# Fused attention, routed experts and tanh-shrink: the router's pieces at other score blocks, the values' high part on GpSimd

## The chip, the cores and the metric

One NeuronCore of a Trainium2 chip runs the whole program. The metric is the time of one execution on the device, in microseconds; of the kernel before there are three such times and one profiled execution. PE is TensorE, DVE VectorE, ACT ScalarE, POOL GpSimd, SP the engine that issues most DMAs.

## The reference, cut to what matters

```python
def _attn_ref(q, k, v):                     # B, H, S, D = 4, 8, 1152, 64
    q_pool = q.reshape(B, H, S // 2, 2, D).mean(axis=3)
    scores = 1/sqrt(D) * np.matmul(q_pool, k.transpose(0, 1, 3, 2))
    scores = scores - np.max(scores, axis=-1, keepdims=True)
    attn = np.exp(scores); attn = attn / (np.sum(attn, axis=-1, keepdims=True) + 1e-09)
    return np.matmul(attn, v)
...
x = attn_out.transpose(0, 2, 1, 3).reshape(2304, 512)
do_compute = x @ w_skip > 0                 # the router: which tokens, and which expert
e_idx = np.argmax(x @ w_gate, axis=1)
...
y = x + gate_w * (relu(x @ w1[e]) @ w2[e])  # 8 experts
h = y @ w_in; out = (h - np.tanh(h)) @ w_out
```

The change lies wholly in the attention and in the router's share of it.

## The kernel before

**Batches and steps.** The 32 heads are worked off as 16 pairs, n = 0 to 15. `Attention.run` (L426) gives each pair one batch of 18 steps; a step is one block of 128 keys of one head (`st` in the code). In a step TensorE first does the twelve short matmuls of `av` (L299) for the block of six steps earlier (`LAG = 6`), then the two score matmuls of `exact` (L247, L248), at steps 1, 6, 10 and 15 the short score matmuls of `rest` for the last 64 queries, then 0 to 2 matmuls of `maxu` (L187, each 384 keys wide), which find the row maxima for the pair two batches ahead. `MAXU` says how many in which step.

**Who reads what.** ScalarE turns each score block into `ph` (f16, L236) and `p` (f32, L237). GpSimd, in 14 of the 18 steps, makes the low part `pl = p - ph` (L242); VectorE does it in the four steps of `DVE_LO`. VectorE also reduces every `maxu` result (L188). Each pair's inputs are prepared one or two batches ahead by steps that the table `PREP` sets: `v1b`, the high part of the values (`vh = f16(1024 v)`, 128x1152) at step 6, and `v2b`, the low part (`vl = 1024 v - vh`, L153 on VectorE) at step 9; `k2b`, the same of the keys, near step 15. `ENG` says which engine does which. VectorE's preparations wait in the list `bg`, and `behind` takes one after each `maxu`.

**Rings of buffers.** Score blocks rotate through three PSUM buffers (`ps_ex`). Another three (`ps_mx`) are shared by everything else: the `maxu` results, the transposed row maxima of `maxrow2` (L216) and the router's two pieces. A tile of that ring can be written when the tile three places earlier has been read.

**The router's pieces.** When a pair's output is complete (step 5 of the next batch, then four VectorE instructions taken one by one behind the `maxu`), `on_pair` appends the router's pieces of that pair to the list `todo`, which happens in step 7. They are: `first` (four transposes, L545, copied to `r_xt` by ScalarE, L548); in every second quarter of the work, where a pair touches five token tiles in place of four, one more `first` of one transpose (copied by VectorE, L550); `second` (L555: four or five matmuls, two records each in the trace, then VectorE's L560 or L558); and some DMAs of SP (zeros into `ys`, rows of x to `xd`). At the end of each step, one piece is taken if the step is in `SIDE`:

```python
if self.todo and st in (self.LASTSIDE if n == NP - 1 else self.SIDE):
    self.todo.pop(0)()
```

```python
MAXU = (2, 0, 2, 1, 1, 2, 1, 2, 1, 2, 2, 1, 2, 1, 1, 2, 2, 2)
SIDE = (3, 4, 5, 8, 13, 17)
PREP = {-6: ("q1",), -4: ("k1b",), -3: ("k2b",), -1: ("kt",), 0: ("q2",), 1: ("q3",), 2: ("qt",),
        4: ("kc",), 6: ("v1b",), 9: ("v2b",)}
```

So before, in a four-tile batch (pairs 0 to 3 and 8 to 11, whose pieces run in batches 1 to 4 and 9 to 12), `first` is in step 8 and `second` in step 13; in a five-tile batch (5 to 8 and 13 to 15) the pieces are in steps 8, 13 and 17. After the attention come `route`, the experts and the dense layer; their code is the same in both kernels.

Of the kernel before, what the change touches and what calls it, by code (L numbers as in the profile page):

```python
# [27 lines left out]
class Attention:  # L28
# [62 lines left out]
    def prep(self, n, i):  # L91
        if n >= self.NP:
            return
        nc, s, eng = self.nc, self.st[n], self.ENG.get((n, i)) or self.ENG.get(i)
        if i == "q1":
# [215 lines left out]
            self.final(n, h)  # L311

    AVG = (3, 5)
    SIDE = (3, 4, 5, 8, 13, 17)
    LAST_LO = (0, 1, 2, 4, 6, 9, 10, 11, 13, 14, 16, 17)
    LAST_HI = (0, 1, 2, 5, 7, 9, 12, 14, 16)
    LO0 = (9, 10, 12, 13, 14, 16)
# [2 lines left out]
    def final(self, n, h):  # L320
# [17 lines left out]
        if h == 1 and self.on_pair:  # L338
# [4 lines left out]
    PREP = {-6: ("q1",), -4: ("k1b",), -3: ("k2b",), -1: ("kt",), 0: ("q2",), 1: ("q3",), 2: ("qt",),  # L343
            4: ("kc",), 6: ("v1b",), 9: ("v2b",)}

    ENG = {"k1b": "act", "k2b": "dve", "v1b": "act", "v2b": "dve", "k10": "act", "k11": "act", "k20": "dve", "k21": "dve", "q1": "pool", "q2": "act", "q3": "dve",
# [85 lines left out]
    def run(self):  # L432
# [5 lines left out]
        for n in range(NP):  # L438
            for st in range(18):
# [25 lines left out]
                if st == (self.ROW[1] if n else self.ROW0[2]):  # L465
                    self.maxrow2(n + 1)
                if self.todo and st in (self.LASTSIDE if n == NP - 1 else self.SIDE):
                    self.todo.pop(0)()
# [21 lines left out]
class Router:  # L490
# [27 lines left out]
    def setup(self):  # L518
# [13 lines left out]
        for a in range(2):  # L532
            G.memset(self.least[:, a:a + 1], float(max(j for b, j in Experts.SIDE if b == a) + 1))

# [248 lines left out]
class Experts:  # L783
# [6 lines left out]
    SX, S1, S2 = 2.0 ** 8, 2.0 ** 4, 2.0 ** 8  # L790
    SIDE = {(0, 1): 2, (0, 2): 2, (0, 3): 2, (0, 4): 2, (1, 1): 2, (1, 2): 2, (1, 3): 2}

# [10 lines left out]
    def setup(self, ctx, inv, wide):  # L803
# [8 lines left out]
        self.groups, i = {}, 0  # L812
        for k, n in self.SIDE.items():
            self.groups[k] = list(range(i, i + n))
# [451 lines left out]
```

## Time and profile before

| | |
|---|---|
| median of 3 runs | 1055.69 us (1053.09 to 1057.06) |
| profiled execution, its own time | 1054.1 us |
| its span, first to last instruction | 1052.5 us |
| PE busy | 944.3 us (90%) |
| DVE busy | 788.6 us (75%) |
| ACT busy | 649.2 us (62%) |
| POOL busy | 543.1 us (52%) |

The shares of the whole span are averages over stages. The attention takes up about the first 460 us, and there the slices of the profile show ScalarE at 9 tenths, PE at 9, VectorE at 8 and 9, GpSimd at 7 and 8; in the dense layer at the end PE alone is at 9. The chain of waits that ended last is followed back only into the experts (about 600 us), so the attention isn't in it, and is read from its own stretches, batch by batch. A batch begins at the first score matmul (L247, 512 wide) of its step 0: batch 3 at 122.77 us, batch 4 at 148.22, batch 7 at 226.81, batch 8 at 253.12.

### The profile page before, as it was taken

What the parts mean: (1) busy time and instruction counts of PE and PEld (TensorE: products, weight loads), DVE (VectorE), ACT (ScalarE), POOL (GpSimd) and SP (SyncE); (2) the same over time, 40 slices, a digit from 0 to 9 for tenths busy, and PEclk for the clock granted to TensorE, in tenths of its full rate; (3) what the DMA queues carried; (4) which work ended last, traced back from release to release, by engine and by line L of the source; (5) the groups of instructions that cost most, each with busy time, mean ns of one, the idle gap of its engine ahead of it and who ended that gap; (6) DMA issues with size and microseconds to landing.
All of it is one profiled execution on the core that took longest, in us unless ns stands there. A gap on an engine that the chain in (4) does not pass through costs nothing. (4 is left out here: it accounts for less than half of the span.)

```text
span 1052.5 us, 25432 instructions
## 1 busy us (share of the span) xinstructions
PE 944.3 (90%) x10249; PEld 703.9 (67%) x10249; DVE 788.6 (75%) x1420; ACT 649.2 (62%) x1224; POOL 543.1 (52%) x478
## 2 busy tenths in 40 slices
PE   5688999999999999948879775999999999999998
PEld 2355666666666666636657453778888888888886
DVE  8677888888888899867979953877666666666654
ACT  4586999999999998835444351444444444444443
POOL 8855888777888887523645622242332323223221
PEclk8898999999999999978989987999999999999999
DMA  7764878855575630039647352211111211212100
GB/s 221 145 155 123 225 185 176 202 125 126 129 180 126 134 99 15 27 127 358 221 162 284 123 190 99 78 50 42 60 52 40 71 41 40 61 31 70 21 21 21
DMA packets 129795, 122.50 MB, mean 116 GB/s; under 512 B 92270, under 2 KB 96878, under 8 KB 128622
## 3 DMA queue, kind: packets, MB, share of 16 engines
q1 hardware_dynamic: 121934, 92.74, 34.0%
q0 software_dynamic: 7712, 27.79, 7.5%
q8 instruction: 91, 1.49, 0.6%
q14 instruction: 58, 0.48, 0.2%
HBM read 74.73 MB, written 19.14 MB: 89 GB/s over the span
## 5 line engine op out<-in xcount | busy, mean ns | idle before, releaser
L242 POOL TENSOR_TENSOR pl<-p,ph 128x512 f16<-128x512 f32 x214 | 265.4, 1258 | 80.6 <-ACT p L237 64.2
L188 DVE TENSOR_REDUCE m<-ps_m 128x1 f32<-128x384 f32 x432 | 222.8, 546 | 32.3 <-PE ps_m L187 30.5
L1095 POOL TENSOR_TENSOR gl<-v,gh 128x512 fp32r<-128x512 f32 x71 | 92.1, 1298 | 271.6 <-ACT gh L1094 267.6
L236 ACT ACTIVATE ph<-ps_e 128x512 f16<-128x512 f32 x279 | 184.3, 660 | 57.2 <-PE ps_e L248 56.0
L1094 ACT CAST gh<-v 128x512 fp32r<-128x512 f32 x72 | 44.5, 618 | 190.1 <-DVE v L1093 190.1
L299 PEld LDWEIGHTS <-ph 128*128 128x128 f16 x2304 | 133.2, 99 | 42.6 <-issue 15.5
L1078 PE MATMUL ps_ch<-xT,wi 128*128 128x256 f16 x576 | 159.0, 276 | 0.7 <-ACT xT L1062 0.7
L1079 PE MATMUL ps_ch<-xT,wi 128*128 128x256 f16 x576 | 158.3, 275 | 0.5 <-DVE xT L1063 0.4
L1080 PE MATMUL ps_ch<-xT,wi 128*128 128x256 f16 x576 | 158.3, 275 | 0.0
L187 PE MATMUL ps_m<-ks,qT 128*128 128x384 f16 (+1 forms) x480 | 124.7, 339 | 24.3 <-DVE m L188 16.3
L237 ACT ACTIVATE p<-ps_e 128x512 f32<-128x512 f32 x211 | 142.7, 676 | 0.0
L299 PE MATMUL ps_a<-vh,pl 128*128 128x65 f16 x1152 | 136.4, 195 | 0.0
L299 PE MATMUL ps_a<-vh,ph 128*128 128x65 f16 x1152 | 136.3, 195 | 0.0
L299 PE MATMUL ps_a<-vl,ph 128*128 128x65 f16 x1152 | 136.2, 195 | 0.0
L1089 DVE SCALAR_TENSOR_TENSOR v<-u,ps_ch 128x512 f32<-128x512 f32 x72 | 49.3, 685 | 113.5 <-ACT t L1087 103.0
L1111 PE MATMUL ps_co<-wo,gh 128*128 128x512 f32 x288 | 119.7, 416 | 0.0
L1113 PE MATMUL ps_co<-wo,gl 128*128 128x512 f32 x288 | 114.0, 396 | 1.0 <-POOL gl L1095 1.0
L247 PE MATMUL ps_e<-qT,ks 128*128 128x512 f16 x288 | 111.2, 386 | 4.0 <-ACT p32r L237 2.0
L248 PE MATMUL ps_e<-qT,kh 65*128 65x512 f16 x288 | 111.6, 388 | 3.4 <-DMA qT<-mt 3.4
L1112 PE MATMUL ps_co<-wo,gh 128*128 128x512 f32 x288 | 113.6, 394 | 0.0
L299 PEld LDWEIGHTS <-pl 128*128 128x128 f16 x1152 | 108.2, 98 | 0.0
L187 PEld LDWEIGHTS <-qT 128*128 128x128 f16 (+1 forms) x480 | 42.2, 102 | 77.0 <-issue 43.9
(222 smaller groups left out, 2158.2 us busy)
## 6 DMA issues: line engine op xcount, KB each, us to landing
v<-in_v_dram SPq DMA_DIRECT2D x16, 576.0 KB
k<-in_k_dram SPq DMA_DIRECT2D x15, 576.0 KB
q<-in_q_dram SPq DMA_DIRECT2D x16, 512.0 KB
raw<-in_moe_w_in_dram SPq DMA_DIRECT2D x8, 1024.0 KB
w1f<-in_moe_w_dram POOLq DMA_DIRECT2D x8, 1024.0 KB, 7.1
w2f<-in_moe_w_dram POOLq DMA_DIRECT2D x8, 1024.0 KB, 8.1
raw<-in_moe_w_out_dram SPq DMA_DIRECT2D x8, 1024.0 KB
ys<-zero SPq DMA_DIRECT2D x5, 1280.0 KB
```

The lines of the kernel that those rows point to most:

```text
L187: nc.tensor.matmul(ps[o, 0:384], w, ks[:, h, c * 384:(c + 1) * 384], start=True, stop=True)
L188: nc.vector.tensor_reduce(out=s["m2"][:, i, c:c + 1], in_=ps[:, 0:384], axis=AX.X, op=ALU.max)
L236: nc.scalar.activation(ph, ps, AF.Exp, scale=2.0 ** -20)
L237: nc.scalar.activation(src, ps, AF.Exp, scale=2.0 ** -20)
L242: (nc.vector if dve else nc.gpsimd).tensor_tensor(out=pl, in0=src, in1=ph, op=ALU.subtract)
L299: self.nc.tensor.matmul(o, x, r, start=first and i == 0, stop=k == NKT - 1 and i == 2, skip_group_check=True)
L1078: nc.tensor.matmul(ps[:, a], self.wi[0][:, w], xh[:, c], start=c == 0, stop=False)
L1079: nc.tensor.matmul(ps[:, a], self.wi[0][:, w], xl[:, c], start=False, stop=False)
L1080: nc.tensor.matmul(ps[:, a], self.wi[1][:, w], xh[:, c], start=False, stop=c == 3)
L1111: nc.tensor.matmul(o, gh[:, a, s], self.wo[0][:, w], start=f == 0, stop=False)
L1112: nc.tensor.matmul(o, gh[:, a, s], self.wo[1][:, w], start=False, stop=False)
L1113: nc.tensor.matmul(o, gl[:, a, s], self.wo[0][:, w], start=False, stop=f == 15)
```

## The change

Two tables of `Attention` change. `SIDE` names other steps, and `v1b` is given to GpSimd (`high` then issues L144, a `tensor_scalar` with the output as before, in place of ScalarE's L140).

```diff
-    SIDE = (3, 4, 5, 8, 13, 17)
+    SIDE = (3, 5, 7, 10, 13, 17)
...
-    ENG = {"k1b": "act", "k2b": "dve", "v1b": "act", "v2b": "dve", "k10": "act", ...
+    ENG = {"k1b": "act", "k2b": "dve", "v1b": "pool", "v2b": "dve", "k10": "act", ...
```

`v1b` without a number for the half is issued in batches 1 to 13, so thirteen instructions move from ScalarE to GpSimd. The pieces of the router go to steps 7 and 10 in a four-tile batch, and to 7, 10 and 13 in a five-tile batch; DMA pieces that followed in step 17 or in step 3 of the next batch now come in 13 and 17.

GpSimd in batch 3, steps 3 to 8 (`pl` and `rl` are low parts of probabilities, `vh` the values' high part), as a piece of the difference:

```order
 L242 TENSOR_TENSOR pl<-p_2373,ph 128x512
+L144 TENSOR_SCALAR vh_144<-v_1582 128x18x64
 L242 TENSOR_TENSOR pl<-p_2399,ph 128x512
 L242 TENSOR_TENSOR pl<-p_2430,ph 128x512
 L242 TENSOR_TENSOR rl_0_159<-p32r,rh_0_158 128x256
```

The new instruction stands between the low parts of steps 4 and 5.

VectorE in batch 3, steps 8 to 13, before (`m_2056` takes the maxima of the pair two ahead, `m_2682` those of the pair after it; `lg` are the router's logits):

```order
L188 TENSOR_REDUCE m_2056<-ps_m 128x1 x3
L153 SCALAR_TENSOR_TENSOR vl_147<-v_1581,vh_144 128x18x64
L188 TENSOR_REDUCE m_2056<-ps_m 128x1 x2
L242 TENSOR_TENSOR rl_1_157<-ps_l,rh_1_156 128x320
L188 TENSOR_REDUCE m_2056<-ps_m 128x1 x2
L188 TENSOR_REDUCE m_2682<-ps_m 128x1
L208 TENSOR_REDUCE mm<-m_2056 128x9
L558 TENSOR_TENSOR lg<-ps_r,lg 128x36
```

And after the change:

```order
L188 TENSOR_REDUCE m_2062<-ps_m 128x1 x3
L153 SCALAR_TENSOR_TENSOR vl_147<-v_1582,vh_144 128x18x64
L188 TENSOR_REDUCE m_2062<-ps_m 128x1
L558 TENSOR_TENSOR lg<-ps_r,lg 128x36
L188 TENSOR_REDUCE m_2062<-ps_m 128x1
L242 TENSOR_TENSOR rl_1_157<-ps_l,rh_1_156 128x320
L188 TENSOR_REDUCE m_2062<-ps_m 128x1 x2
L188 TENSOR_REDUCE m_2688<-ps_m 128x1
L208 TENSOR_REDUCE mm<-m_2062 128x9
```

The reading of `second` (L558) moves from behind the last maximum to right behind the first reduction that follows `vl`.

TensorE in batch 3 (it multiplies with `vh_142`), step 10, as a piece of the difference (`second` is new there):

```order
 L187 LDWEIGHTS qT
 L187 MATMUL ps_m<-ks,qT 128x384
+L555 MATMUL ps_r<-w_81,r_xt 128x9 x4
 L299 LDWEIGHTS ph
 L299 MATMUL ps_a<-vh_142,ph 128x65
```

And step 13 of the same batch, where it is taken away:

```order
 L187 LDWEIGHTS qT
 L187 MATMUL ps_m<-ks,qT 128x384
-L555 MATMUL ps_r<-w_81,r_xt 128x9 x4
 L299 LDWEIGHTS ph
 L299 MATMUL ps_a<-vh_142,ph 128x65
```

In step 10 it stands behind two `maxu` matmuls, in step 13 it stood behind one.

## Rows read from the trace of the kernel before

**Rows 1.** Busy time by stretch: batches 3, 6, 13; us (instructions) of PE, PEld, DVE, ACT, POOL; TensorE's clock, DMA share, GB/s.
```profile
122.77:148.22 25.45, 24.26 (x392) 16.87 (x388) 22.25 (x47) 23.94 (x49) 21.77 (x19) 1.00 0.80 191
...
200.50:226.81 26.31, 24.88 (x394) 17.15 (x391) 23.04 (x48) 24.04 (x48) 21.04 (x19) 1.00 0.54 123
...
380.83:409.38 28.55, 25.56 (x420) 17.81 (x417) 27.60 (x60) 24.06 (x49) 21.02 (x19) 1.00 0.35 85
```

**Rows 2.** Waits in 97.43 to 380.83 (batches 2 to 12): us, times, longest.
```profile
POOL pl L242 <- ACT p L237: 33.2, 59, 1.1
...
PE ps_m L187 <- DVE m L188: 10.2, 18, 1.2
...
PE ps_e L247 <- ACT p32r L237: 1.4, 4, 0.4
```

**Rows 3.** Timeline of TensorE, batch 3, steps 12 to 14: start, us, instruction [idle before].
```profile
139.27 0.35 PE L187 MATMUL ps_m<-ks,qT 128*64 128x384 f16 x2
140.19 0.35 PE L187 MATMUL ps_m<-ks,qT 128*64 128x384 f16 x2 [0.57 <-DVE m L188]
140.86 0.38 PE L247 MATMUL ps_e<-qT,ks 128*128 128x512 f16 x1
...
141.52 1.06 PE L555 MATMUL ps_r<-w,r_xt 128*128 128x9 f32 x8
142.44 0.19 PE L299 MATMUL ps_a<-vh,ph 128*128 128x65 f16 x1
...
142.80 0.38 PE L247 MATMUL ps_e<-qT,ks 128*128 128x512 f16 x1
```

**Rows 4.** Timeline of VectorE, batch 3, steps 10 to 17.
```profile
137.33 2.35 DVE L153 SCALAR_TENSOR_TENSOR vl<-v,vh 128x1152 f16<-128x1152 f32 x1
139.60 1.01 DVE L188 TENSOR_REDUCE m<-ps_m 128x1 f32<-128x384 f32 x2
...
142.62 0.20 DVE L558 TENSOR_TENSOR lg<-ps_r,lg 128x36 f32<-128x36 f32 x1
143.60 0.56 DVE L188 TENSOR_REDUCE m<-ps_m 128x1 f32<-128x384 f32 x1 [0.78 <-PE ps_m L187]
...
147.57 1.41 DVE L153 SCALAR_TENSOR_TENSOR kn<-k,kn 128x1152 f16<-128x1152 f32 x1
```

**Rows 5.** Timeline of TensorE, step 0 of batch 4.
```profile
149.51 0.32 PE L187 MATMUL ps_m<-ks,qT 128*128 128x384 f16 x1 [0.53 <-DVE m L188]
```

**Rows 6.** Timeline of TensorE, step 17 of batch 7 (five tiles).
```profile
251.16 1.28 PE L555 MATMUL ps_r<-w,r_xt 128*128 128x9 f32 x10 [0.41 <-DVE m L188]
```

**Rows 7.** Groups of GpSimd, shapes apart, whole span: xcount | busy us, mean ns | idle before.
```profile
L144 POOL TENSOR_SCALAR vh<-v 128x576 f16<-128x576 f32 x2 | 1.3, 673 | 0.2
```

**Rows 8.** Groups of instructions, batches 2 to 12.
```profile
L140 ACT ACTIVATE vh<-v 128x1152 f16<-128x1152 f32 x11 | 13.7, 1243 | 0.0
```

**Rows 9.** Timeline of GpSimd, batch 3, steps 2 to 10.
```profile
128.35 5.92 POOL L242 TENSOR_TENSOR pl<-p,ph 128x512 f16<-128x512 f32 x5 [0.19 <-ACT p L237]
...
137.30 3.38 POOL L242 TENSOR_TENSOR pl<-p,ph 128x512 f16<-128x512 f32 x2 [0.32 <-ACT p L237]
```

**Rows 10.** Line 153 in 95 to 445 us: duration ns min/median/max, first and last start.
```profile
L153 DVE SCALAR_TENSOR_TENSOR kn<-k,kn x12: 1341/1419/1677, 96.6 to 380.6; 128x1152 f16<-128x1152 f32 x12
...
L153 DVE SCALAR_TENSOR_TENSOR vl<-v,vh x12: 1539/2342/2349, 111.9 to 396.6; 128x1152 f16<-128x1152 f32 x12
```

**Rows 11.** Timeline of SP, batch 3.
```profile
137.16 0.50 SPq L168 DMA_DIRECT2D kh<-ks  x1
145.03 0.81 SPq L225 DMA_DIRECT2D qT<-mt  x1
```

**Rows 12.** Busy time in 88 to 95 us.
```profile
88.00:95.00 7.00, 7.00 (x61) 5.02 (x61) 3.43 (x11) 4.29 (x9) 2.08 (x2) 0.50 0.08 29
```

**Rows 13.** Timeline of TensorE, batch 1, step 13.
```profile
87.60 1.71 PE L555 MATMUL ps_r<-w,r_xt 128*128 128x9 f32 x8
```

**Rows 14.** Timeline of TensorE, step 14 of batch 14.
```profile
428.69 0.27 PE L216 MATMUL ps_t<-ident,mm 128*9 128x128 f32 x1 [1.29 <-DVE mm L208]
```

More of the change, by code (lines that the diff above doesn't have):

```diff
@@ L344 @@
             4: ("kc",), 6: ("v1b",), 9: ("v2b",)}
-    ENG = {"k1b": "act", "k2b": "dve", "v1b": "act", "v2b": "dve", "k10": "act", "k11": "act", "k20": "dve", "k21": "dve", "q1": "pool", "q2": "act", "q3": "dve",
+    ENG = {"k1b": "act", "k2b": "dve", "v1b": "pool", "v2b": "dve", "k10": "act", "k11": "act", "k20": "dve", "k21": "dve", "q1": "pool", "q2": "act", "q3": "dve",
            "v10": "act", "v11": "act", "v20": "dve", "v21": "dve", (0, "k11"): "act", (0, "k21"): "pool",
```

## The prediction

> **What bounds the kernel now.** The change touches the attention alone, so I read the attention batch by batch: first the busy time of each engine in whole batches, then the list of waits over batches 2 to 12, then the timelines of single steps.
>
> A four-tile batch lasts 25.45 us, and in it TensorE is busy for 24.26, ScalarE 23.94, VectorE 22.25, GpSimd 21.77 [rows 1]. All four are nearly full, so the question is who makes whom wait. The list of waits answers it: TensorE waits 10.2 us for the reductions of VectorE (L188) and 1.4 us for ScalarE, while GpSimd waits 33.2 us for ScalarE's results [rows 2]. TensorE sets the pace, at its full clock of 1.00 [rows 1], and loses time where the three buffers of the ring `ps_mx` are all unread. GpSimd has the most room: 25.45 less 21.77 is 3.68 us a batch.
>
> The timelines show where the ring fills. In step 10 VectorE starts `v2b` (vl, 2.35 us), and the reductions behind it start only at 139.60 [rows 4]. TensorE runs on to step 12, places the first pair of L187 at 139.27 and must wait 0.57 us for the second [rows 3]. The same happens in step 0 of the next batch, 0.53 us [rows 5], behind the keys' low part at 147.57 [rows 4]. A five-tile batch lasts 26.31 us [rows 1]; there `second` has ten matmul records, stands in step 17 and waits 0.41 us itself [rows 6].
>
> **The change, part by part.**
>
> *`second` in a four-tile batch, from step 13 to step 10.* Its matmuls take 142.44 less 141.52, so 0.92 us [rows 3]. In step 10 they delay steps 11 and 12 by that, and then TensorE meets the same reductions later. The ring has turned by one tile: the first pair of step 12 now needs the buffer that the second pair needed, and comes at 139.27 + 0.92 = 140.19, which is when that buffer came free before [rows 3]. The second pair needs the buffer of `second`, which L558 (0.20 us [rows 4]) empties right behind that reduction, at about 140.3; the pair comes a pair later (modelled 0.35), at 140.5. So the wait of 0.57 is filled with work that used to stand in step 13. Step 13 begins at 140.86 + 0.92 - 0.57 = 141.21 and is 0.92 shorter: step 14 begins 0.57 earlier. VectorE can follow, since it waited 0.78 us for TensorE just there [rows 4]. The wait in step 0 [rows 5] moves along with the keys' low part and stays. There are seven such batches (2 to 4 and 9 to 12; 25.34 to 25.45 us long): 7 x 0.57 = 4.0 us. Bounds: 0, if VectorE can't follow, and 7 x (0.57 + 0.53) = 7.7, if both waits go.
>
> *Five-tile batches (5 to 8).* Step 10 takes the one transpose, too short to fill the wait, so the first pair of step 12 waits until 140.19 and the second follows 0.35 later. Then `second`, 1.28 less 1.06 longer than the four-tile one [rows 3, 6], stands in step 13 as it does in a four-tile batch now. Such a batch should last 25.45 + 0.35 + 0.22 = 26.02 where it lasted 26.31: 4 x 0.29 = 1.2 us. Bounds: 0 and 4 x (0.29 + 0.57).
>
> *Batch 1.* There `second` ran at a granted clock of 0.50, 1.2 GHz [rows 12], and took 1.71 us [rows 13]. In step 10 it runs at 1.00 and stands ahead of a pile of thirteen L187 that wait for VectorE anyway. The slow stretch ends when it ends, so what comes up in its place is slowed too; I take half of 1.71, 0.85 us (bounds 0 and 1.71).
>
> *Batches 13 to 15.* Batch 13 is VectorE's: 27.60 of 28.55 us busy [rows 1], so at most 0.95 is there; I take 0.4. In step 14 of batch 14 TensorE waits 1.29 us for the row maxima [rows 14]; the five-tile `second`, some 1.1 us, now stands ahead of that wait in step 13; I take 0.6. Together 1.0 (bounds 0 and 0.95 + 1.29).
>
> *`v1b` from ScalarE to GpSimd, thirteen times.* ScalarE loses 1.24 us a batch [rows 8]. TensorE waits for ScalarE only 1.4 us in eleven batches [rows 2], so I take no gain; the bounds are 0 and 13 x 1.24 = 16. GpSimd has never done 1152 columns of this; half as many took 0.67 us [rows 7], so at most 1.35, which the idle 3.68 us cover. Behind it wait the low parts of steps 5 and 6, about 1.3 us later; they were ready near 134.3 [rows 9] and are multiplied six steps after their scores, six times 25.45 / 18 or 8.5 us, so no one notices. `v2b` needs its result at 137.33 [rows 4]; GpSimd makes it from about 131.9, after three of the five low parts that begin at 128.35 [rows 9]. Without that cover the full 1.35 would come on the path, 17.6 us in all.
>
> VectorE's low part of the values takes a median of 2.34 us where the keys' takes 1.34 at best, and the former starts 0.03 us after a low part of GpSimd [rows 4, 9, 10]; both read two tensors from SBUF. The Trainium skill (GPSIMD Engine Reference, "Key points") says that GpSimd shares its SBUF interfaces with VectorE and contends with its instructions that have two SBUF inputs. By that rule `v1b` costs VectorE only if it meets such an instruction; at 131.9 to 133.3 VectorE reduces from PSUM, and the sum stays. Charging VectorE with all of it would give 17.6 us against the change.
>
> *DMAs.* Zero fills and x rows move past L225, the row of maxima, on SP's queue. They wait for nothing late, and between the end of L168's issue and L225 SP has 7.4 us free [rows 11]; nothing is charged.
>
> Sum: 4.0 + 1.2 + 0.85 + 1.0 = 7.05 us off the profiled execution's 1054.1, so 1047.0. The median of the runs shown is 1.6 above that execution; on its scale the forecast is 1048.6, and all times below are on it.
>
> **The rivals.** About 0.5%, 5.3 us, is what a measurement of this kernel can tell from no change; "faster" means below 1050.4.
>
> 1. *VectorE gives nothing back.* If VectorE, not the ring, is the limit from step 10 to step 0, the 0.57 reappears as a longer wait in step 0. For it: all of TensorE's waits end with VectorE [rows 2]. Against it: its idle 0.78 us in between [rows 4]. Only the last terms stay, 1.85: 1053.8.
>
> 2. *`v1b` frees VectorE.* If the delayed GpSimd starts its low part of step 9 behind the start of `v2b`, that instruction falls from 2.35 toward 1.54, its best [rows 10], by 0.8 us. In four-tile batches nothing waits any more; in the four others the wait of 0.57 goes too, 2.3 us, and about half a microsecond each in batches 1 and 13: 1045.3. It takes a `v1b` close to 1.4 us. The Trainium skill's rule above (GPSIMD Engine Reference, "Key points") is what would do it; the spread of 1.54 to 2.35 agrees [rows 10].
>
> 3. *ScalarE was the limit.* It has 1.5 us of idle time in a batch [rows 1]. If TensorE's waits only hid its queue, the 1.24 us come back too, thirteen times a good half of it, some 9 us more: 1039.6. Against it stand the 1.4 us of waits.
>
> 4. *GpSimd becomes the limit: slower.* With 3.68 us of idle time less the 0.57 that a batch gets shorter, it decides from a `v1b` of about 3.1 us, and beyond 3.7 the batch is longer than before. At 4.5 us a batch takes 21.77 + 4.5 = 26.27, 0.82 more than now, 10.7 in thirteen: 1066.4. Only a price of 3.3 times twice the 0.67 of the half [rows 7] would do it.
>
> That the change does less than it says is rival 1 in effect: the pieces aren't spread over more blocks in a four-tile batch, they stand in two as before, three blocks apart.
>
> **How the numbers follow.** Forecast 0.52, rivals 0.22, 0.11, 0.08 and 0.07 in that order. The forecast's own range is 1044.5 to 1052, by the bounds of its terms; a tenth of it or more lies above 1050.4. Faster: 0.9 x 0.52 + 0.11 + 0.08 = 0.66; the same: 0.05 + 0.22 = 0.27; slower: 0.07. The range leaves out the slow rival and the far end of rival 3: 1040 to 1056.
>
> **What would show it.** Right: four-tile batches of some 24.9 us and five-tile ones of 26.0; no wait of TensorE in step 12 of the former; L555 in step 10; L144 of 1.1 to 1.35 us with GpSimd's waits for ScalarE smaller; step 0 still waiting some 0.5. Wrong: a wait of over 1 us in step 0, L144 over 3 us, or a `vl` much shorter than 2.3 us, which is rival 2.

## The result, and the profile after

The changed kernel takes 1044.53 us (median of 4 runs, 1043.07 to 1046.08) where the kernel before, in the same comparison, takes 1055.74 (4 runs): a ratio of 0.9905, 95% interval [0.9882, 0.9928]. The forecast was 1048.6 in a range of 1040 to 1056: faster, as forecast, by 4 us more. The profiled execution of the changed kernel took 1046.08 us and is the longest of its four, so the two profiles differ by 8.0 us where the medians differ by 11.2. The kernel before has only four executions in that comparison; in the next one it has 22, with a median of 1054.28, and against that the difference is 9.8.

The first part of the page (busy time of each engine) and, from a list of groups with shapes apart, the moved instruction (xcount | busy us, mean ns | idle before):

```profile
PE 941.9 (90%) x10249; PEld 704.6 (67%) x10249; DVE 788.5 (75%) x1420; ACT 641.4 (61%) x1211; POOL 557.1 (53%) x491
```
```profile
L144 POOL TENSOR_SCALAR vh<-v 128x1152 f16<-128x1152 f32 x13 | 15.0, 1156 | 1.1
```

Thirteen instructions went from ACT to POOL, at 1.16 us each, and VectorE's sum is the same to 0.1 us. Busy time by stretch, batches 3, 6 and 13 (columns as in [rows 1]):

```profile
119.33:144.02 24.69, 24.16 (x391) 16.82 (x388) 22.14 (x47) 23.22 (x48) 22.84 (x20) 1.00 0.77 193
194.92:221.14 26.22, 24.44 (x395) 17.18 (x392) 23.19 (x48) 23.53 (x48) 22.14 (x20) 1.00 0.63 135
372.31:401.10 28.79, 25.69 (x421) 17.89 (x417) 26.42 (x58) 23.48 (x48) 19.94 (x19) 1.00 0.30 65
```

Against [rows 1] the four-tile batch is 0.76 us shorter, the five-tile one only 0.09, and batch 13 is 0.24 longer. The waits in batches 2 to 12, against [rows 2]:

```profile
POOL pl L242 <- ACT p L237: 13.7, 26, 0.9
PE ps_m L187 <- DVE m L188: 10.4, 15, 1.2
...
PEld ps_r L555 <- DVE m L188: 1.4, 4, 0.3
```

GpSimd's waits for ScalarE's `p` fell from 33.2 to 13.7 us and TensorE's wait for ScalarE is gone, but TensorE waits for VectorE's maxima as long as before (10.2 and 10.4). The total hides a shift, which the timeline of TensorE shows: batch 3 from step 10 on (three rows), step 12 of batch 7, step 0 of batch 8, and batch 13 (the last three):

```profile
133.45 0.95 PE L555 MATMUL ps_r<-w,r_xt 128*128 128x9 f32 x8
...
136.77 0.52 PE L187 MATMUL ps_m<-ks,qT 128*64 128x384 f16 x4
138.04 0.33 PE L187 MATMUL ps_m<-ks,qT 128*128 128x384 f16 x1
...
238.91 0.55 PE L187 MATMUL ps_m<-ks,qT 128*64 128x384 f16 x4 [0.52 <-DVE m L188]
...
249.27 0.32 PE L187 MATMUL ps_m<-ks,qT 128*128 128x384 f16 x1 [1.15 <-DVE m L188]
...
387.92 0.33 PE L545 MATMUL ps_r<-ident,x_all 128*128 128x128 f32 x1 [0.44 <-DVE m L188]
...
391.26 0.35 PE L187 MATMUL ps_m<-ks,qT 128*64 128x384 f16 x2 [0.65 <-DVE m L188]
392.15 0.35 PE L187 MATMUL ps_m<-ks,qT 128*64 128x384 f16 x2 [0.54 <-DVE r_xt L550]
```

In the four-tile batch both pairs of step 12 follow each other without a wait, where there was one of 0.57 [rows 3]. In the five-tile batch the first pair of step 12 still waits, and step 0 behind it waits 1.15 us, where batches 6 to 8 before waited under 0.1 in step 0. A wait of that length was there before the change too, in step 0 of batches 5 and 13, where no `second` stands in step 17 ahead of it; this is batch 5 before:

```profile
175.58 0.32 PE L187 MATMUL ps_m<-ks,qT 128*128 128x384 f16 x1 [1.15 <-DVE m L188]
```

Batch 13 after the change has three waits in steps 10 and 12, one of them for the extra `first` that VectorE copies (L550).

What doesn't move with the steps is `vl`, which stands in front of the maxima. VectorE and GpSimd in batch 3:

```profile
133.96 2.30 DVE L153 SCALAR_TENSOR_TENSOR vl<-v,vh 128x1152 f16<-128x1152 f32 x1
136.18 0.54 DVE L188 TENSOR_REDUCE m<-ps_m 128x1 f32<-128x384 f32 x1
136.65 0.18 DVE L558 TENSOR_TENSOR lg<-ps_r,lg 128x36 f32<-128x36 f32 x1
```
```profile
128.67 1.16 POOL L144 TENSOR_SCALAR vh<-v 128x1152 f16<-128x1152 f32 x1
...
132.77 4.50 POOL L242 TENSOR_TENSOR pl<-p,ph 128x512 f16<-128x512 f32 x3
```

`vl` lasts 2.30 us here (2.35 in [rows 4]); three low parts of GpSimd that need 3.39 us elsewhere need 4.50 beside it.

**Where the 8.0 us between the two profiles are** (from the starts of the batches, the last matmul of the attention, the first one of the experts and the first one of the dense layer, L1078): batches 0 and 1, 78.2 to 75.4 us; batches 2 to 13, 312.0 to 306.5; batches 14 and 15, no change; from the last L299 to the first L889, which is the routing, 22.5 to 20.5; experts, 172.9 to 175.2; dense layer, 400.6 to 400.5. A part that the prediction didn't name, the routing, gave 2.0 us.

### The profile page after: what moved, and what is told of

The parts are those of the page before. It is cut to its first block, busy times and chain, and to the rows that moved or that the text cites. A ratio compares the mean times of both kernels' runs of the same rounds, so it can differ in the third digit from the quotient of the medians.

```text
span 1044.6 us, 25445 instructions
## 1 busy us (share of the span) xinstructions
PE 941.9 (90%) x10249; PEld 704.6 (67%) x10249; DVE 788.5 (75%) x1420; ACT 641.4 (61%) x1211; POOL 557.1 (53%) x491
## 5 line engine op out<-in xcount | busy, mean ns | idle before, releaser
L188 DVE TENSOR_REDUCE m<-ps_m 128x1 f32<-128x384 f32 x432 | 225.5, 548 | 37.4 <-PE ps_m L187 34.7
L236 ACT ACTIVATE ph<-ps_e 128x512 f16<-128x512 f32 x279 | 177.0, 635 | 57.5 <-PE ps_e L248 54.2
L299 PEld LDWEIGHTS <-ph 128*128 128x128 f16 x2304 | 133.4, 99 | 49.7 <-issue 22.6
L1078 PE MATMUL ps_ch<-xT,wi 128*128 128x256 f16 x576 | 158.7, 275 | 0.7 <-ACT xT L1062 0.7
L187 PE MATMUL ps_m<-ks,qT 128*128 128x384 f16 (+1 forms) x480 | 122.7, 338 | 23.9 <-DVE m L188 16.1
L299 PE MATMUL ps_a<-vh,ph 128*128 128x65 f16 x1152 | 136.7, 195 | 0.0
L299 PE MATMUL ps_a<-vh,pl 128*128 128x65 f16 x1152 | 136.6, 195 | 0.0
L299 PE MATMUL ps_a<-vl,ph 128*128 128x65 f16 x1152 | 136.5, 195 | 0.0
L237 ACT ACTIVATE p<-ps_e 128x512 f32<-128x512 f32 x211 | 134.5, 637 | 0.0
L299 PEld LDWEIGHTS <-pl 128*128 128x128 f16 x1152 | 108.4, 98 | 0.0
L187 PEld LDWEIGHTS <-qT 128*128 128x128 f16 (+1 forms) x480 | 42.9, 102 | 68.1 <-issue 34.3
```

The costliest lines, as they stand in the source:

```text
L187: nc.tensor.matmul(ps[o, 0:384], w, ks[:, h, c * 384:(c + 1) * 384], start=True, stop=True)
L188: nc.vector.tensor_reduce(out=s["m2"][:, i, c:c + 1], in_=ps[:, 0:384], axis=AX.X, op=ALU.max)
L236: nc.scalar.activation(ph, ps, AF.Exp, scale=2.0 ** -20)
L237: nc.scalar.activation(src, ps, AF.Exp, scale=2.0 ** -20)
L299: self.nc.tensor.matmul(o, x, r, start=first and i == 0, stop=k == NKT - 1 and i == 2, skip_group_check=True)
L1078: nc.tensor.matmul(ps[:, a], self.wi[0][:, w], xh[:, c], start=c == 0, stop=False)
```

## The experiments

Each row below is one kernel. "Pieces" says in which steps the router's pieces run, "vh" which engine makes the high part of the values. Ratios are to the kernel before on the same chip. Lengths are from the profile: a four-tile and a five-tile batch (batches 3 and 6 or 7; in the kernel before the five-tile batches 5 and 8 take 26.84 and 26.04), batch 13, batches 2 to 13 together, and the routing (last L299 to first L889).

| kernel | pieces | vh | ratio, 95% interval | four | five | 13 | 2 to 13 | routing |
|---|---|---|---|---|---|---|---|---|
| before | old | ACT | 1 | 25.45 | 26.31 | 28.55 | 312.0 | 22.5 |
| the change | new | POOL | 0.9905 [0.9882, 0.9928] | 24.69 | 26.22 | 28.79 | 306.5 | 20.5 |
| side_only | new | ACT | 0.9970 [0.9953, 0.9986] | 24.81 | 26.45 | 28.21 | 307.7 | 22.5 |
| v1b_only | old | POOL | 0.9969 [0.9951, 0.9987] | 25.47 | 26.34 | 29.63 | 313.3 | 21.0 |
| five_early | new, own for five | POOL | 0.9845 [0.9818, 0.9873] | 24.69 | 25.55 | 27.14 | 302.4 | 19.7 |
| maxu_moved | new | POOL | 0.9901 [0.9879, 0.9923] | 24.68 | 25.88 | 28.45 | 304.8 | 20.4 |
| both | new, own for five | POOL | 0.9818 [0.9792, 0.9843] | 24.68 | 25.04 | 26.79 | 299.7 | 20.6 |
| five_early_act | new, own for five | ACT | 0.9891 [0.9864, 0.9918] | 24.81 | 25.55 | 27.01 | 302.7 | 22.4 |
| both_act | new, own for five | ACT | 0.9902 [0.9872, 0.9932] | 24.80 | 25.04 | 26.68 | 300.4 | 21.9 |
| side_from2 | new from batch 2 | POOL | 0.9929 [0.9903, 0.9955] | 24.70 | 26.22 | 28.80 | 306.6 | 20.7 |
| v1b_dve | new | DVE | 0.9911 [0.9884, 0.9938] | 24.75 | 25.55 | 28.50 | 303.9 | 22.5 |
| dve_only | old | DVE | 0.9920 [0.9889, 0.9951] | 24.70 | 25.60 | 28.88 | 304.2 | 23.0 |
| both_dve | new, own for five | DVE | 0.9883 [0.9852, 0.9913] | 24.75 | 25.17 | 27.78 | 301.7 | 22.6 |
| v2b_late | new | POOL | 1.0049 [1.0029, 1.0068] | 25.91 | 26.20 | 31.86 | 317.9 | 20.6 |

**The two edits apart.** `side_only` is the changed kernel with `"v1b": "act"`, `v1b_only` the kernel before with `"v1b": "pool"`.

> The changed kernel with v1b back on ScalarE (only SIDE is new). Theory A (the gain comes from 0.9 us of second's matmuls filling TensorE's wait in step 12, v1b is neutral): four-tile batches of 24.7 to 24.9 us as in the changed kernel, no wait in step 12, time within 3 us of the changed kernel (1042 to 1048). Theory B (ScalarE was the limit and the gain is v1b's): four-tile batches back at about 25.4 us, time within 2 us of the kernel before.

> The kernel before with v1b on GpSimd (SIDE is old). Theory A: four-tile batches stay at 25.4 us with the wait of 0.57 in step 12 and the time is within 2 us of the kernel before. Theory B: the batches shorten by up to 1 us each, the time by 8 to 13 us. If v1b disturbs the low parts of GpSimd (the slow rival) the time rises above that of before.

Medians of 1050.9 and 1051.39 where the kernel before has 1054.28. In the batches the steps do nearly all: with them alone, batches 2 to 13 go from 312.0 to 307.7, and the high part on GpSimd adds 1.2; with the old steps it gives the batches nothing (313.3, since batch 13 is 1.1 longer). The five-tile batch of `side_only` (26.45) is no shorter than before. In ratios the two don't add up: 3 and 3 us apart, 10 together; with intervals of 2 us and more either way, most of that gap may be noise. By the batches theory A holds in both; by the time no theory holds: 1050.9 lies above theory A's 1048, and 1051.39 is 2.9 us under the kernel before, where theory A allowed 2. The routing, which no theory had, gives `v1b_only` 1.5 of these 2.9.

**Own steps for the five-tile batches.** The wait in their step 12 was not filled, because only the one transpose stands in step 10; `five_early` puts `second` there.

```diff
+    SIDE5 = (3, 5, 7, 8, 10, 17)
...
-    if self.todo and st in (self.LASTSIDE if n == NP - 1 else self.SIDE):
+    if self.todo and st in (self.LASTSIDE if n == NP - 1 else self.SIDE5 if n > 4 and (n - 1) // 4 % 2 else self.SIDE):
```

> The changed kernel with the pieces of five-tile batches in steps 7, 8 and 10 in place of 7, 10 and 13, so that second's ten matmul records (1.12 us) and not one transpose follow v2b's start. Theory A: the five-tile batches fall from 26.22 us to about 25.0 and lose the wait in step 12, in all 4 x 1.2 = 5 us less than the changed kernel, plus up to 1 us in batches 13 and 14: 1038 to 1040. If VectorE is the limit in five-tile batches whatever the order (it reads one more tile), they stay above 26 and the time stays at 1044.

Measured 1039.02 us. TensorE's timeline in step 12 of batch 7 has no wait left, and the windows of batches 7 and 13:

```profile
236.26 0.52 PE L187 MATMUL ps_m<-ks,qT 128*64 128x384 f16 x4
```
```profile
217.96:243.51 25.55, 24.30 (x395) 16.90 (x391) 23.08 (x48) 23.44 (x48) 22.16 (x20) 1.00 0.61 128
367.83:394.97 27.14, 25.41 (x420) 17.65 (x417) 25.60 (x58) 23.48 (x48) 19.96 (x19) 1.00 0.32 69
```

0.67 us in each of four batches and 1.65 in batch 13: 4.3 us by the batches, some 6 by the ratio. The time is theory A's, but by another sum: the five-tile batches stay at 25.55, not 25.0, and batch 13 gives more than was expected. What was filled is the wait that the prediction had left standing, and by the means that it described for the four-tile batches. The longer wait in step 0 is still there, in batch 8:

```profile
245.43 0.32 PE L187 MATMUL ps_m<-ks,qT 128*128 128x384 f16 x1 [1.16 <-DVE m L188]
```

**The wait in step 0.** One matmul of the maxima goes from step 0 to step 1.

```diff
-    MAXU = (2, 0, 2, 1, ...
+    MAXU = (1, 1, 2, 1, ...
```

> The changed kernel with one maxu moved from step 0 to step 1 (MAXU begins 1, 1 in place of 2, 0), so that its buffer has been read when it comes. Theory A (the ring behind k2b makes the wait of step 0, VectorE has room): the wait of 0.53 us in step 0 goes (1.3 in five-tile batches), batches shorten by 0.6 to 0.7 us, in all 7 to 10 us less than the changed kernel: 1035 to 1038. If VectorE is the limit from v2b to step 2, the wait reappears in step 1 or 2 and the time stays at 1044.

Measured 1044.07. The wait in step 0 is gone (0.69 us in four-tile batches with the pauses around it), and steps 1 and 2 of those are as much longer, 0.47 and 0.21 us, with new waits for ScalarE of 0.30 and 0.18 us. The waits of TensorE in batches 2 to 12:

```profile
PE ps_l L247 <- ACT p L237: 3.3, 11, 0.3
PE ps_m L187 <- DVE m L188: 2.6, 4, 0.7
PE ps_e L247 <- ACT p32r L237: 2.0, 11, 0.2
```

The four-tile batch keeps its 24.68: ScalarE takes the place of the ring there, so the time is that of the second theory, but the engine behind it isn't VectorE. Only the five-tile batches, whose step 0 waited longer, gain (0.34). Both edits together:

> The kernel with its own steps for the five-tile batches and with one of the maxima's matmuls moved from step 0 to step 1. Moved alone it took away the wait of step 0, which came back in steps 1 and 2, so that four-tile batches kept their 24.68 us and five-tile ones went from 26.22 to 25.88. Theory A (VectorE is behind from the keys' low part on, and both edits take the same wait of the five-tile batches): four-tile batches 24.7, five-tile ones 25.5 to 25.6, batch 13 near 27.1, and a median of 1038 to 1040, as with the first edit alone. Theory B (the waits of step 0 and of step 12 are two): five-tile batches of 25.2 or less and a median of 1036 to 1038.

Measured 1035.13, the best of all: 0.9818 of the kernel before, about 9 us under the change. In the windows of batches 3, 7 and 13 the five-tile batch is 25.04, within 0.36 of a four-tile one; the two waits were two, so theory B is right for them.

```profile
116.81:141.49 24.68, 24.19 (x392) 16.82 (x389) 22.12 (x47) 23.23 (x48) 22.83 (x20) 1.00 0.77 192
216.23:241.27 25.04, 24.46 (x395) 16.98 (x392) 23.04 (x48) 23.22 (x48) 22.11 (x20) 1.00 0.60 131
365.01:391.80 26.79, 25.58 (x420) 17.71 (x417) 25.48 (x58) 23.37 (x48) 19.93 (x19) 1.00 0.32 70
```

**What the high part on GpSimd is worth.** `five_early_act` and `both_act` are those two kernels with `"v1b": "act"`.

> The kernel with its own steps for the five-tile batches, and the values' high part back on ScalarE. In the medians so far the two edits apart gave 3.4 and 2.9 us and both together some 10; in the batches of the profiles the high part on GpSimd is worth 0.12 us in a four-tile batch (24.81 against 24.69) and 0.23 in a five-tile one (26.45 against 26.22), and batch 13 gives 0.6 back. Theory A (what the batches show is all there is): four-tile batches back at 24.81, batches 2 to 13 together 1 to 2 us longer than the 302.4 us with GpSimd, and a median of 1040 to 1042, where it was 1039.0 with GpSimd. Theory B (the two edits need each other somewhere outside of those batches, as the medians suggest): a median of 1044 to 1046, with the loss before batch 2 or behind the attention.

> The same kernel with the values' high part on ScalarE, where the kernel before had it. In it the waits left in steps 1 and 2 are for ScalarE (0.46 and 0.36 us a batch). Theory A (the high part on GpSimd is worth what the batches show): batches up to 0.3 us longer than with GpSimd's 24.68 and 25.04, 1 to 3 us in thirteen, and a median of 1036 to 1038 where GpSimd gave 1035.1. Theory B (it is worth more, outside of those batches, as the medians of the other pairs, 3 to 6 us, suggest): a median of 1039 to 1042 with batches that are hardly longer.

Medians of 1041.46 and 1042.56. In batches 2 to 13 ScalarE costs 0.3 and 0.8 us more than GpSimd, even less than theory A has it; the ratios differ by 0.0046 and 0.0084, some 5 and 9 us with intervals of about 4 us either way, which is theory B's side. (The medians alone put the first, 1041.46, into theory A's range.) Part of what lies outside the batches can be seen. GpSimd at the end of the attention, before and after the change (L836 starts a load of expert weights, L845 the gather of the first expert's rows):

```profile
470.44 0.97 POOL L836 DMA_DIRECT2D w1f<-in_moe_w_dram  x1 [17.27 <-DVE slot L700]
471.71 1.05 POOL L845 DMA_INDIRECT bx<-xd,inv  x1 [0.17 <-issue]
```
```profile
458.61 0.97 POOL L836 DMA_DIRECT2D w1f<-in_moe_w_dram  x1 [13.70 <-DVE kf L608]
459.59 0.12 POOL L695 MEMSET inv<- 128x2 int32 x1
462.21 1.04 POOL L845 DMA_INDIRECT bx<-xd,inv  x1 [2.50 <-DVE slot L700]
```

Before, the load is issued 17.3 us after GpSimd's last low part, and the gather, which the experts wait for, only behind it. After, the load goes out 3.6 us earlier, and the gather as soon as VectorE has made its addresses (`inv`, L699, just ahead of L700). The instructions and their order there are the same. L700 in the first line is the profile's guess and no cause: after the change the same load starts before L700. In all seven kernels that have the high part on GpSimd the idle time is 13.7 us and the routing 19.7 to 21.0; in all seven others it is 17.0 to 17.6 and 21.9 to 23.0, whichever of ScalarE and VectorE has it. In these seven an 8 KB transfer of the instruction queue starts 1.8 to 2.4 us before the late load, in the first seven 1.4 to 1.8 us after it, where GpSimd waits for the addresses anyway. In the late seven the gather starts 1.2 to 1.8 us after L700 ends, in the first seven always 0.21 us after it. Of `side_only`, from 457.7 to 461.6 us, the DMA queues show:

```profile
q1 hardware_dynamic: 324, 0.82, 53.9%
q14 instruction: 1, 0.01, 0.5%
```

So with thirteen instructions more ahead of that place GpSimd doesn't stop before the load, which is worth 2.0 us between the two kernels: the gather is 1.2 us earlier against L700, and the first expert matmul 0.7 earlier against the gather, which isn't explained. That the stop is a wait for instructions to arrive is read from the coincidence of fourteen profiles and isn't shown; no kernel tested it by adding instructions that do nothing.

**Batch 1.** The changed kernel with the old steps in batches 0 and 1:

```diff
-    ... else self.SIDE):
+    ... else self.SIDE if n > 1 else (3, 4, 5, 8, 13, 17)):
```

> The changed kernel with the old steps for the pieces in batches 0 and 1 alone. Theory A (batch 1 is 5.2 us shorter since the router's second piece moved out of its half-clock stretch): batch 1 back at about 35 us, batch 0 as it was, batch 2 beginning near 97 to 99 us, and a median 3 to 5 us over the 1044.5 of the change. Theory B (batches 0 and 1 scatter with where the half-clock stretches fall, since batch 0, whose code is the same, moved by 2.3 us as well): batch 2 begins between 94 and 97.5 us, batch 1 has the waits of the kernel before in its own steps, and the median is within 2 us of 1044.5. Batches 2 to 13 should be as in the change in both, 306.5 us together.

Measured 1045.55, and batch 1 takes 29.61 us, as in the change (30.01): theory B, though batch 2 begins at 93.64, just ahead of its 94. Over all profiles batch 1 takes 29.6 to 35.2 us with its old steps (four kernels) and 28.4 to 31.9 with the new ones (ten), and batch 0, which the edits hardly touch, 43.0 to 45.4. Both kernels have a granted clock of 0.50 (1.2 GHz) near 20 to 27 and 34 to 41 us; then the kernel before has it once more, from 84.8 to 95.0 us, the change twice, from 58.2 to 65.1 and from 85.6 to 89.0. With the old steps batch 1 is the longer the more of it is at clock 0.50: 29.61 us with 3.4 of them, 31.43 with 7.2, 31.73 with 7.4, 35.21 with 10.2 (the kernel before). So the 5.2 us that batch 1 lost between the two profiles can't be put down to the steps, and what these are worth there can't be told.

**The high part on VectorE.** `v1b_dve` is the change with `"v1b": "dve"`, `dve_only` the kernel before with it, `both_dve` the best kernel with it.

> The changed kernel with the values' high part on VectorE, where half of it took 0.73 us, so 1.46 for the whole. It tells what a microsecond of VectorE costs in a batch. Theory A (VectorE sets the pace between the waits of TensorE for its reductions; its idle time elsewhere can't be used): four-tile batches grow by 0.7 to 1.46 us, to 25.4 to 26.1, and the thirteen batches by 9 to 19 us: a median of 1054 to 1063. Theory B (only the ring's two places matter, and VectorE catches up between step 6 and step 10): four-tile batches stay within 0.3 us of 24.69, and the median within 4 us of 1044.5.

> The kernel before (old steps for the router's pieces) with the values' high part on VectorE. In the profiles so far each low part of keys or values on VectorE (L153, 1152 columns) ends 1.21 or 1.22 us after the end of the low part that GpSimd has in hand when it starts, so its length is set by where in GpSimd's instruction it starts; with the high part on VectorE and the new steps, it was 1.46 us in place of 2.30 and 2.12, and the wait of the five-tile batches in step 12 was gone. Theory A (the wait of step 12 is the length of vl, and the pieces only filled it): with vl near 1.5 the old steps lose it too; four-tile batches of 24.8 to 25.0 us, where they had 25.44, five-tile ones of 25.4 to 25.9, where they had 26.3, no wait over 0.3 us in step 12, and a median of 1045 to 1049. Theory B (the wait comes of where the pieces stand): four-tile batches stay at 25.4, five-tile ones at 26.3, and the median at 1051 to 1054.

> The kernel with its own steps for the five-tile batches, with one of the maxima's matmuls moved from step 0 to step 1, and with the values' high part on VectorE in place of GpSimd. Theory A (VectorE has room, since vl is shorter by most of what the high part takes): four-tile batches 24.6 to 24.8 us, five-tile ones 24.9 to 25.1, a median of 1034 to 1037, as with the high part on GpSimd (1035.1). Theory B (without the wait of step 0 VectorE's sum of about 22.7 and 23.8 us a batch is what is left): batches longer by 0.3 or more each, and a median of 1039 or above.

Medians of 1043.5, 1045.41 and 1041.14. `v1b_dve` is theory B's: VectorE gets an instruction more in every batch, and the four-tile batches are only 0.06 longer for it, while its five-tile batches fall from 26.22 to 25.55, and `dve_only`, with the old steps, has batches 2 to 13 in 304.2 us, less than the whole change. The windows of batches 3 and 7 of `dve_only`, then its VectorE and TensorE in batch 3 (step 12 is the four L187):

```profile
121.03:145.80 24.77, 24.13 (x392) 16.88 (x389) 22.49 (x48) 23.30 (x48) 22.13 (x19) 1.00 0.87 197
222.12:247.70 25.58, 24.71 (x394) 17.10 (x391) 22.98 (x49) 23.38 (x47) 21.38 (x19) 1.00 0.58 131
```
```profile
131.76 1.39 DVE L142 TENSOR_SCALAR vh<-v 128x1152 f16<-128x1152 f32 x1
...
135.77 1.35 DVE L153 SCALAR_TENSOR_TENSOR vl<-v,vh 128x1152 f16<-128x1152 f32 x1
```
```profile
137.78 0.52 PE L187 MATMUL ps_m<-ks,qT 128*64 128x384 f16 x4
```

`vl` takes 1.35 us in place of 2.35, so VectorE's sum is 22.49 where it was 22.25, and the wait of step 12 is gone with the old steps too: theory A. Only in batch 13 `vl` takes 2.33 us again, and there step 12 waits 0.83. That wait is the length of `vl`; the new steps had only filled it. `both_dve` falls between its theories: the median is theory B's and the four-tile batches theory A's, but batch 13, where VectorE is busiest, is 1.0 longer than in `both`, five-tile ones 0.13, and the routing 2.0, as wherever GpSimd lacks the thirteen instructions. Batches and routing make 4.0 of the 6 us by which it is slower than `both`.

**`vl` two reductions later.** The changed kernel with one step changed:

```diff
-            4: ("kc",), 6: ("v1b",), 9: ("v2b",)}
+            4: ("kc",), 6: ("v1b",), 10: ("v2b",)}
```

> The changed kernel with the low part of the values (vl) called for in step 10 in place of step 9, which puts it two reductions later in VectorE's order, behind the reading of the router's second piece. Theory A (TensorE's waits follow vl): vl lasts between 1.25 and 2.4 us and ends 1.22 us after the low part that GpSimd has in hand when it starts; the wait of 0.68 us in step 12 of the five-tile batches moves to a later step or goes; four-tile batches of 24.5 to 24.9 us, five-tile ones of 25.5 to 26.2, and a median of 1041 to 1045. Theory B (the wait belongs to step 12's two matmuls, whatever vl does): step 12 still waits 0.6 us or more in the five-tile batches, which stay at 26.2, and the median is that of the change, 1043 to 1046.

Measured 1058.14 us, 1.0049 [1.0029, 1.0068] of the kernel before and 14 us above the change; both theories missed the time. The wait did follow `vl`: step 12 of the five-tile batches has none, and `second` in step 13 waits the 0.52 that step 12 had. But in four-tile batches `vl` now meets GpSimd's L99 and is long again (VectorE, GpSimd and TensorE, batch 3):

```profile
137.90 2.36 DVE L153 SCALAR_TENSOR_TENSOR vl<-v,vh 128x1152 f16<-128x1152 f32 x1
```
```profile
137.63 1.41 POOL L99 TENSOR_TENSOR qs<-q 128x576 f32<-128x576 f32 x1
```
```profile
141.18 0.32 PE L187 MATMUL ps_m<-ks,qT 128*128 128x384 f16 x1 [0.57 <-DVE m L188]
142.29 0.27 PE L216 MATMUL ps_t<-ident,mm 128*9 128x128 f32 x1 [0.79 <-DVE mm L208]
```

The last maxima now stand behind it. In step 14 the matmul of the maxima waits for a buffer, and the row maxima (L208) that TensorE transposes there come late: a chain that had no wait in the change. Four-tile batches are 1.2 longer than in the change, batch 13 3.1.

## Why the prediction was right, point by point

- **The direction and the place were right.** The waits of TensorE behind VectorE's `vl` were the thing to fill, and `second` in step 10 fills the one of step 12 in the four-tile batches. The prediction's term was 0.57 a batch, 4.0 in seven; measured are 0.76 and 5.1. The steps alone give 0.64 (`side_only`), the high part another 0.12, which the prediction set at 0.
- **The five-tile term failed in part**: 1.2 forecast, 0.6 measured, of which 0.6 is batch 5 alone and the other three gain 0.01 together (the prediction took 26.31 for all four, where batches 5 and 8 had 26.84 and 26.04). The wait of step 12 stays, as stated. The step that failed is the next one, "as it does in a four-tile batch now": step 0 waits 1.15 us there, not the 0.53 of [rows 5], since the keys' low part starts later (0.27 us before step 0, against 0.64) and takes 1.67 us in place of 1.42. What makes it start later isn't located. Before, `second` in step 17 had stood in front of that wait and filled it in batches 6 to 8, so moving it away opened a wait elsewhere. Step 0 of batch 5 showed its length before the change; [rows 5] is of batch 4.
- **Batches 13 to 15**: 1.0 forecast, and 0.3 longer measured (batch 13 0.24 longer, batch 14 0.26 shorter, batch 15 0.30 longer). The step "at most 0.95 is there; I take 0.4" failed: VectorE's idle time rose to 2.4 us there, but TensorE's waits for VectorE in steps 10 to 13 of batch 13 only moved. They were 0.50 and 1.12 us before and are 0.44, 0.65 and 0.54 after, the last of them for L550 in the middle of a pile of maxima.
- **Batch 1**: 0.85 forecast, 5.2 shorter in the profile, with 2.3 of it given back in batch 0; `side_from2` shows that the steps there are not needed for it. No run tells whether this term is right.
- **`v1b` at nothing** was right for VectorE and GpSimd: L144 takes 1.16 us (1.1 to 1.35 forecast), and no one waits for it. As a term of the sum it was wrong by 1.2 us in the batches and by 2.0 in the routing, which the prediction didn't look at because its code is the same.
- **The sum is in part luck.** It was 7.05 us, and the profiles place 7.4: 5.1 in the four-tile batches, 0.6 in the five-tile ones, -0.3 in batches 13 to 15 and 2.0 in the routing. The second and third of these are 1.9 short of the forecast, the first is 1.1 over it, batch 1 can't be told from scatter, and the routing, which wasn't in the sum, made up for the rest.
- **Rivals.** 1 fell: VectorE gives the time back in four-tile batches. 2 has the right mechanism, with another cause than `v1b` on GpSimd: `vl` stays at 2.30 and 2.12 us in the change, but where it is shortened (`dve_only`) the waits go as the rival said. 3 fell in its size: 1.2 us came back in the batches, about the 1.4 us of waits that stood against it. 4 fell: 1.16 us against the 3.1 that it needs.
- **What stays open.** The ratios make the high part on GpSimd worth 3 to 9 us in four pairs of kernels, with intervals of 2 to 4 us either way; batches and routing show 0.2 to 3.2. The rest, if it is more than noise, lies in the start, the experts or the dense layer and isn't located: these differ by 4 to 6 us over the fourteen profiles (batch 2 begins at 91.8 to 97.4 us, the experts take 171.0 to 176.4, the dense layer 398.8 to 402.8). In the same way the 7.4 us that are placed stand against 9.8 to 11.2 by the medians.

## What to carry to other kernels

A wait at a ring of buffers belongs to what the reader does ahead of it: ask first why that instruction takes twice its best time, since shortening it (`dve_only`) is worth as much as a schedule that fills the wait. When a piece of work is moved to fill a wait, look at what it filled where it stood. And compare the stages that aren't changed too: with more or fewer instructions ahead of it, an engine may issue its next DMAs earlier or later.

## What the runs showed of the hardware

**VectorE's two-input instructions and GpSimd's take turns.** In 353 of the 364 low parts of keys or values of 1152 columns (L153, fourteen profiles) the instruction ends 1.20 to 1.23 us after the end of the GpSimd instruction that is in hand when it starts, whatever its own length between 1.35 and 2.4 us; in five others no GpSimd instruction was running, and they took 1.34 to 1.36 us. GpSimd's next low part, when it follows at once, then takes 2.27 us in place of 1.16. In four of the rest the instruction started 0.05 us before the GpSimd one ended and ended 2.33 us after that end, behind the next GpSimd instruction. In batch 3 of the change GpSimd's part in hand ended at 135.04 and `vl` at 136.26; in batch 3 of `v1b_dve` at 131.42 and 132.63. So the price of such an instruction is set by the phase: up to 1.1 us on each side, or nothing for VectorE when it starts some 0.14 us ahead of the other's end (1.35 us in `dve_only`). VectorE's low parts that read PSUM (0.68 us) show none of this. The Trainium skill (SBUF — State Buffer, "SBUF: two separate sides") calls the shared pair of ports "an exclusive lock, not a bandwidth split"; these rows agree. The prediction had this mechanism for `vl` in rival 2, at a chance of 0.11; its forecast left `vl` at its length and filled the wait behind it.

**VectorE's one-input conversion waits as well.** L142 on VectorE (values from f32 to f16) ends 0.62 or 0.63 us after the GpSimd part in hand, and takes 0.83 to 1.46 us accordingly, in 39 of 39 instructions of three profiles. GpSimd's L144, the same work, always takes 1.16 us (91 of 91); beside it VectorE ran almost only reductions and products that read PSUM, never an L142 or L153.

**A stop in GpSimd's own program** goes when thirteen instructions are put ahead of it, as told with the routing above. From the last instruction that prepares the load to the load itself it is 0.67 us in the seven profiles without it and 3.7 to 4.3 in the seven with it, so the stop takes 3.0 to 3.6 us. Its cause isn't shown.
